# A fused adaLN, linear-attention and SwiGLU block: K-V state folded into the output projection, per-tile transposes, and the output projection spread over the first FFN chunk

## The chip, the cores and the metric

The kernel runs on one core of one Trainium2 chip. The metric is device time in microseconds (us). "Fast" runs are those within 1.5% of the fastest run of the same kernel; all times compared below are of fast runs.

The engines are TensorE (PE: matmuls; PEld: its weight loads, which overlap with matmuls, as 862.9 and 413.4 us of the two fit into a span of 915.7 in the kernel before), VectorE (DVE), ScalarE (ACT), GpSimd (POOL) and SyncE (SP, which issues most DMA here: 171 of the 235 issues of the kernel before). "Granted clock" (PEclk) is the share of full speed that the throttle gave TensorE. These kernels put matmul results into PSUM tiles, called banks here (a wide matmul's is 128x512 in f32); to evict one is to copy it out with another engine. A wide matmul is one with 512 columns.

## The reference

The input x is 2048 x 1024, and w_gate and w_up are 1024 x 3584. There are 32 heads of width 32. Everything is stored in bf16.

```python
mod = silu(c) @ w_mod                       # six rows of 1024: sa, ca, ga, sb, cb, gb
h = layernorm(x) * (1 + ca) + sa
q, k, v = split(h @ wqkv)
phi = lambda t: where(t > 0, t + 1, exp(t)) + 1e-6
kv  = einsum('bhsd,bhse->bhde', phi(k), v);  z = phi(k) summed over s
o   = (phi(q) @ kv) / (phi(q) . z + 1e-6)   # per head
x = x + ga * (o @ wo)
h = layernorm(x) * (1 + cb) + sb
x = x + gb * ((silu(h @ w_gate) * (h @ w_up)) @ w_down)
```

The order of the stages is forced. All of kv and z must be known before any output row. Each output row needs wo, then the second layer norm, then a transpose for the next matmul, and then the FFN.

## The kernel before

The 2048 rows are 16 tiles of 128, in 4 chunks of 512. In the first phase each chunk does a layer norm, K, V, Q and an update of kv. Then each tile does `nd` (numerator and denominator), a division, a transpose of o, the projection with wo, and the second layer norm. Tiles 4 to 15 are interleaved with gate and up of FFN chunk 0. The rest is an FFN stream.

```python
def emit_nd(st):                    # phi(q) @ [kv | z]: 8 matmuls, 132 columns
    ...
    nc.vector.reciprocal(out=rd[:], in_=rd[:])
    ...                             # o_sb = numerator * rd
def emit_tp(o_sb, st):              # 8 transposes of o, one eviction
    ...
def emit_wo(st, oT_t):
    ...                             # a_ps = oT_t @ wo (16 matmuls), x1 = x + a_ps, bn_stats
    nc.gpsimd.tensor_scalar(out=xn2[:], in0=x1_t[:], scalar1=rstd[:], scalar2=nmr[:], ...)
    xn2_lists.setdefault(sc, []).append(xn2)          # only collected here
    ...
    elif t == STC - 1:              # transposes when the chunk's four tiles are there
        transpose_chunk_to(h2T_c, xn2_lists[sc], cb1T, sbT, ...)

def p456_iter(i):                   # three tiles in flight
    o_tiles[i + 2] = emit_nd(i + 2)
    oT_tiles[i + 1] = emit_tp(o_tiles.pop(i + 1), i + 1)
    emit_wo(i, oT_tiles.pop(i))
...
interleave(ffn_gate_up_iter(0, gu_pool, psum_gu), list(range(STC, ST)))
```

## Time and profile before

| kernel before | us |
|---|---|
| median of 4 runs (beside the changed kernel) | 915.83 (914.19 to 917.9) |
| span of the profiled run | 915.7 |
| TensorE busy | 862.9 (94%) |
| VectorE / ScalarE / GpSimd busy | 303.3 / 212.2 / 58.1 |

TensorE bounds the kernel. Eight 128x512 matmuls take 1.73 us when they run unbroken (216 ns each), and from about 429 us on, the profile is an almost unbroken stream of them. A matmul's own record is longer (379 ns), so successive records overlap. For that reason a group's busy time can be read as a share, but the pace has to be read from the timeline.

The waits view of the kernel before, TensorE only, names the waiting instruction and its releaser, then us in total, times, and the longest.

```profile
PE mT_ps L175 <- DMA wme<-in_w_mod_dram: 18.4, 4, 10.0
PE acc L265 <- DVE pk_c L220: 6.8, 3, 3.3
PE y_ps L534 <- DMA wd_sb<-in_B_w_down_dram: 3.5, 3, 1.6
```

The start costs most: TensorE waits for w_mod, then for evictions of K. Two groups of the kernel before are work that the change removes. The columns are count, busy us, mean ns, and the idle time before them.

```profile
L363 PE MATMUL tp<-ident,o_sb 128*128 128x128 bf16 x128 | 11.3, 225 | 0.9 <-DVE o_sb L353 0.7
L340 PE MATMUL nd<-KVZ,pqT 128*128 128x132 bf16 x128 | 11.2, 226 | 1.3 <-DVE KVZ L312 1.2
```

### The profile page before, as it was taken

To read this page: it belongs to the slowest core of one execution; us is meant where nothing else is said; L and a number is where in the kernel's file an instruction comes from. 1 tells how busy PE (TensorE), PEld (TensorE's weight loads), DVE (VectorE), ACT (ScalarE), POOL (GpSimd) and SP (SyncE) were. 2 spreads that over 40 slices of the span, in tenths; PEclk is the share of its full clock that TensorE was granted. 3 is DMA by queue.
4 is the path that set the end of the run, shared out by engine and by line. 5 is a ranking of instruction groups with operands and counts; after the bars stand their busy time and mean duration, and the time that the engine had idled before them with its cause. 6 is when DMAs were issued, how large, how long until landed. Compare 5 with 4: busy or idle time off the path is not lost.

```text
span 915.7 us, 11358 instructions
## 1 busy us (share of the span) xinstructions
PE 862.9 (94%) x4672; PEld 413.4 (45%) x4760; DVE 303.3 (33%) x568; ACT 212.2 (23%) x362; POOL 58.1 (6%) x109
## 2 busy tenths in 40 slices
PE   1789999997999999998999999999999999999998
PEld 1335464444444544544444444444444444444443
DVE  4745255443665444441121222212212212122222
ACT  3526345342342422313011100111100111110000
POOL 2100000000422122120000000000000000000000
PEclk9999999998999999999999999999999999999999
DMA  9921060031215464459755542454531355511120
GB/s 330 393 104 47 4 227 1 1 92 35 104 66 158 122 184 142 123 151 352 227 153 158 149 127 70 143 158 142 155 110 61 101 157 152 143 48 64 69 69 24
DMA packets 153955, 117.13 MB, mean 128 GB/s; under 512 B 3888, under 2 KB 141104, under 8 KB 153904
## 3 DMA queue, kind: packets, MB, share of 16 engines
q1 hardware_dynamic: 144688, 91.24, 33.0%
q10 hardware_dynamic: 6912, 16.78, 5.8%
q0 software_dynamic: 2304, 8.39, 2.3%
q8 instruction: 37, 0.61, 0.3%
q14 instruction: 14, 0.11, 0.0%
HBM read 103.81 MB, written 12.58 MB: 127 GB/s over the span
## 4 chain that ended last, share of the span: by engine, by line
PE 68%; DMA 3%; DVE 2%; issue 1%; POOL 1%; ACT 1%; SPq 0%; POOLq 0%; DVEq 0%; ACTq 0%
PE y_ps L534 21%; PE u_ps L455 19%; PE g_ps L451 19%; PE a_ps L404 5%; DMA wd_sb<-in_B_w_down_dram 2%; PE tp L363 1%; ACT h2T_c L125 1%; PE nd L340 1%; DVE x_t L406 1%; DMA x_scratch<-x_t 1%; PE tp L121 1%; PE g_ps L398 0%; PE u_ps L226 0%; PE a_ps L398 0%; PE g_ps L226 0%
## 5 line engine op out<-in xcount | busy, mean ns | idle before, releaser
L455 PE MATMUL u_ps<-h2T_c,wu_blk 128*128 128x512 bf16 x877 | 212.1, 379 | 0.9
L451 PE MATMUL g_ps<-h2T_c,wg_blk 128*128 128x512 bf16 x880 | 212.2, 379 | 0.7
L534 PE MATMUL y_ps<-wd_sb,gu 128*128 128x512 bf16 x878 | 195.5, 381 | 4.4 <-DMA wd_sb<-in_B_w_down_dram 3.5
L464 DVE TENSOR_TENSOR gu<-u_ps,sg 128x512 bf16<-128x512 f32 x112 | 77.5, 692 | 296.0 <-PE u_ps L455 266.3
L458 ACT ACTIVATE sg<-g_ps 128x512 f32<-128x512 f32 x112 | 66.9, 598 | 428.8 <-PE g_ps L451 410.8
L534 PEld LDWEIGHTS <-gu 128*128 128x128 bf16 x896 | 88.0, 98 | 111.0 <-issue 6.5
L451 PEld LDWEIGHTS <-wg_blk 128*128 128x128 bf16 x896 | 87.4, 98 | 104.0 <-issue 0.2
L455 PEld LDWEIGHTS <-wu_blk 128*128 128x128 bf16 x896 | 87.3, 98 | 102.9
L265 PE MATMUL acc<-wkv_sb,hT_c 128*128 128x512 bf16 x373 | 88.0, 388 | 7.6 <-DVE pk_c L220 6.8
L537 DVE TENSOR_TENSOR yt<-y_ps,gb_bc 128x512 f32<-128x512 f32 x32 | 22.1, 692 | 155.2 <-PE y_ps L534 155.2
L265 PEld LDWEIGHTS <-hT_c 128*128 128x128 bf16 x384 | 37.5, 100 | 50.7 <-issue 9.9
L219 DVE TENSOR_SCALAR e<-e 128x512 f32<-128x512 f32 x56 | 23.6, 424 | 71.0 <-ACT e L218 71.0
L218 ACT ACTIVATE e<-acc 128x512 f32<-128x512 f32 x56 | 33.2, 603 | 54.4 <-PE acc L226 32.1
L404 PE MATMUL a_ps<-wo_sb,oT_t 128*128 128x512 bf16 x183 | 44.4, 379 | 1.3 <-DVE x_t L406 0.5
L226 PE MATMUL acc<-hT_c,wq_sb 128*128 128x512 bf16 x186 | 42.1, 379 | 0.3
L226 PEld LDWEIGHTS <-wq_sb 128*128 128x128 bf16 x256 | 24.4, 98 | 27.2 <-issue 0.5
L271 ACT CAST v_c<-acc 128x512 bf16<-128x512 f32 x32 | 18.7, 585 | 41.1 <-PE acc L265 39.3
L404 PEld LDWEIGHTS <-oT_t 128*128 128x128 bf16 x192 | 18.2, 97 | 22.2 <-issue 3.1
L265 PE MATMUL acc<-wkv_sb,hT_l 128*128 128x512 bf16 x124 | 28.0, 379 | 0.2
L102 DVE BATCH_NORM_STATS2 stats<-x_sb 128x6 f32<-128x512 bf16 x32 | 21.0, 670 | 9.2 <-DMA x_sb<-in_A_x_dram 9.2
L538 DVE TENSOR_TENSOR ob<-yt,x1r 128x512 bf16<-128x512 f32 x32 | 22.1, 692 | 1.1
L406 DVE TENSOR_TENSOR x_t<-a_ps,x_t 128x512 f32<-128x512 f32 x24 | 16.5, 687 | 17.7 <-PE a_ps L404 17.7
(216 smaller groups left out, 489.7 us busy)
## 6 DMA issues: line engine op xcount, KB each, us to landing
wg_blk<-in_B_w_gate_dram SPq DMA_DIRECT2D x56, 512.0 KB, 3.9
wu_blk<-in_B_w_up_dram SPq DMA_DIRECT2D x56, 512.0 KB, 5.0
wm_blk<-in_w_mod_dram SPq DMA_DIRECT2D x8, 1024.0 KB, 6.0
x_scratch<-x_t POOLq DMA_DIRECT2D x16, 512.0 KB, 3.9
x1r<-x_scratch ACTq DMA_DIRECT2D x16, 512.0 KB, 3.5
wd_sb<-in_B_w_down_dram SPq DMA_DIRECT2D x7, 1024.0 KB, 13.7
x_sb<-in_A_x_dram ACTq DMA_DIRECT2D x16, 256.0 KB, 6.2
wme<-in_w_mod_dram SPq DMA_DIRECT2D x4, 1024.0 KB, 12.4
```

The lines of the kernel that those rows point to most:

```text
L218: nc.scalar.activation(out=e[:], in_=acc, func=ACT.Exp)
L219: nc.vector.tensor_scalar(out=e[:], in0=e[:], scalar1=1.0, scalar2=PHI_EPS, op0=ALU.min, op1=ALU.add)
L226: nc.tensor.matmul(acc[:], lhsT=wq_sb[:, cc, qc * P:(qc + 1) * P], rhs=hT_[:, cc, :], start=(cc == 0), stop=(cc == DC - 1))
L265: nc.tensor.matmul(acc[:], lhsT=hT_c[:, cc, t * P:(t + 1) * P], rhs=wkv_sb[:, cc, n0:n0 + NB], start=(cc == 0), stop=(cc == DC - 1))
L404: nc.tensor.matmul(a_ps[:], lhsT=oT_t[:, cc, :], rhs=wo_sb[:, cc, nb * NB:(nb + 1) * NB], start=(cc == 0), stop=(cc == DC - 1))
L406: nc.vector.tensor_tensor(out=x1_t[:, nb * NB:(nb + 1) * NB], in0=a_ps[:], in1=x_t[:, nb * NB:(nb + 1) * NB], op=ALU.add)
L451: nc.tensor.matmul(g_ps[:, 0:width], lhsT=wg_blk[:, cc, fj * P:(fj + 1) * P], rhs=h2T_c[:, cc, cs], start=(cc == 0), stop=(cc == DC - 1))
L455: nc.tensor.matmul(u_ps[:, 0:width], lhsT=wu_blk[:, cc, fj * P:(fj + 1) * P], rhs=h2T_c[:, cc, cs], start=(cc == 0), stop=(cc == DC - 1))
L458: nc.scalar.activation(out=sg[:, 0:width], in_=g_ps[:, 0:width], func=ACT.Silu)
L464: nc.vector.tensor_tensor(out=gu[:, cs], in0=u_ps[:, 0:width], in1=sg[:, 0:width], op=ALU.mult)
L534: nc.tensor.matmul(y_ps[:], lhsT=guT[sc][f][:, t * P:(t + 1) * P], rhs=wd_sb[:, f, nb * NB:(nb + 1) * NB], start=(f == 0), stop=(f == FC - 1))
L537: nc.vector.tensor_tensor(out=yt[:], in0=y_ps[:], in1=gb_bc[:, nb * NB:(nb + 1) * NB], op=ALU.mult)
```

## The change

The aim is less TensorE work and an earlier start. It does the following:

- It folds the block-diagonal kv into wo once (16 matmuls, `wf`), so that `nd` and the 128 transposes of o disappear. phi(q) is divided by its denominator in place. The denominators of four head groups go into the four 32-column groups of one PSUM bank (`den`), and after a reciprocal, 8 selector matmuls (`bc`) spread them.
- It computes the late modulation rows as wide matmuls with 32 output columns, four column groups to a bank (`modr`).
- It loads x first, then w_mod and the K weights in pieces, and computes K of chunk 0 over six PSUM banks.
- It transposes each tile as soon as its rows are normalised (on VectorE), in both layer norms.
- It gives chunks 1 to 3 of the projection, with their denominators, to the first FFN chunk as side work.

```diff
-    def emit_nd(st): ...
-    def emit_tp(o_sb, st): ...
+    def den_norm(sc):
+        for k in range(2):
+            for g in range(4):
+                nc.tensor.matmul(den[32 * g:32 * g + 32, :], lhsT=Zden[:, 4 * k + g, :], rhs=pq[:, 4 * k + g, :], ...)
+        ...                                   # add eps, reciprocal 128x512, cast
+                nc.tensor.matmul(bc[:], lhsT=Esel[32 * g:32 * g + 32, k, :], rhs=rb[32 * g:32 * g + 32, :], ...)
+                nc.vector.tensor_tensor(out=pq[:, hg, :], in0=bc[:], in1=pq[:, hg, :], op=ALU.mult)
+    ...                                       # wf: wo <- KVT @ wo, 16 matmuls
+    def wo_tile(st):
+        ...                                   # a_ps = pq @ wo (16 matmuls), x1 = a_ps + x_t, bn_stats
+        normalise(xn[:], x1[:], mv[:, 0, 0:1], rstd[:, 0:1])
+        ...
+            pe_transpose_tile(h2Ts[sc], xn, t)        # in the same call
+        if t == STC - 1:
+            ...                               # scale and shift h2T
-        xn2_lists.setdefault(sc, []).append(xn2)
-        elif t == STC - 1:
-            transpose_chunk_to(h2T_c, xn2_lists[sc], cb1T, sbT, ...)
...
+    side = []                                 # wo_tile(4..15), den_norm(2), den_norm(3)
+    for fb in gate_up_blocks(0): ...          # one or two of them after each gate/up block
```

## The prediction

> **What bounds the kernel now.** TensorE: the page gives PE 862.9 of 915.7 us busy (94%), no other engine over 33%. The chain of waits shows eight 128x512 matmuls per 1.73 us (216 ns each); from about 428 to 911 us it is an unbroken stream of FFN matmuls, 2240 x 0.216 = 484 us. The change leaves that stream alone; gain or loss is before 428 us. There the windows show TensorE losing time in three places: 27.5 us idle in the first 60 us (waits view: 18.4 us for w_mod, 6.8 us for pk evictions; DMA full at 350-400 GB/s from 2 to 51 us; first K matmul at 26.4 us); some 10 us between 212 and 240 us, with granted clock 0.83; some 5 us at 430-437 us waiting for wd.
>
> **TensorE work, counted in the instruction order.**
> Removed: nd 128 (11.2 us busy), o transposes 128 (11.3), identity matmuls 8 (1.7), late matvecs 256 and their broadcasts (8.9): 33 us.
> Added (estimates at 216 ns per 512 columns): folded wo 16 (3.5 us), selector broadcasts 4+32 (7.8), KV transposes 8 (0.8), late mod rows 64 and denominators 32 with 32 output columns. If four column tiles run at once, [...] these 96 cost 24 x 0.216 = 5.2 us; if not, 20.7. No trace shows it yet; I expect overlap. Net about -15 us.
>
> **Start.** x comes first, then w_mod and K weights interleaved, 7 MB; pieces with 512 B runs go at about 285 GB/s (wg/wu: 155 GB/s at 0.55 DMA share), landing near 25 us. K of chunk 0 fills six banks as they land, done near 30 us. But chunk 1's normalisation stands ahead of phi on VectorE (about 7 us), and x loads, waiting for buffers, stand ahead of wv in the single SP queue; so K ends near 40 us and V starts near 41. At 69 us I expect about 190 wide matmuls done against 142 before: gain about 11 us.
>
> **Given back.** Before the first FFN: 16 folded-wo evictions on ScalarE (0.6 us each), the chain a_ps, add, BN_STATS, normalise, transpose (3.5-4.5 us) exposed on the last wo tile, then modulation; about 11 us idle, as before. In the first FFN each denominator chain has a 128x512 reciprocal (128x32 takes 351 ns; estimate 4 us), and eight products of 0.69 us pace the broadcasts: about 2 us idle for each of three chunks, plus 0.5-0.7 us at each of 12 transposes. wd should wait 0-2 us. These eat most of the removed work: the stage is about 3 us longer. Late mod: -4; kv evictions with four banks: -2; the rest: about -1.
>
> Sum: -11 +3 -4 -2 -1 = -15 us: **900 us**, range 887 to 914. Chances: faster by over 2% 0.40, within 2% 0.55, slower by over 2% 0.05.
>
> **What would show it.** Right: wide matmuls at 216 ns, the stream after the first down projection as long as before; at least 10 us less idle in the first 60; late-mod and denominator matmuls nearer 54 than 216 ns apart; small waits on pq products and xn transposes; VectorE up by about 50 us to 350.
> Wrong: column tiles at 216 ns (+10 to 15 us); V waiting beyond 45 us for wv; the first FFN over 8 us longer, waiting on VectorE; gate/up waiting for weights because x1r and output DMAs share their queue.
>
> **What would make it wrong.** Another DMA rate at the start, VectorE saturating in the first FFN, or a clock drop after idles (0.83, 0.74 seen before).

The sum: -11 + 3 - 4 - 2 - 1 = -15 us, from 915.7 to about 900. The 5.2 us for 96 overlapping matmuls, in the count of TensorE work, was the expectation; no trace showed it then.

## More of the kernel before

A tile's normalised rows are put on a list, and the transposes of all four tiles of a chunk are emitted only after the projection of the fourth. (What ran stands in places in another order than the source emits it: transposes of `xn_2429` ran at 239.59 us, before the chunk's last projection matmuls at 248.44. So the order is read from the timelines.)

Now the end of one chunk's projection in the timeline of the kernel before. The columns are start, length, engine, line, operation, tiles and count, and in brackets the idle time just before.

```profile
304.58 1.89 PE L404 MATMUL a_ps<-wo_sb,oT_t 128*128 128x512 bf16 x7
306.30 1.24 PE L451 MATMUL g_ps<-h2T_c,wg_blk 128*128 128x512 bf16 x5
307.38 1.89 PE L455 MATMUL u_ps<-h2T_c,wu_blk 128*128 128x512 bf16 x8
309.11 1.03 PE L451 MATMUL g_ps<-h2T_c,wg_blk 128*128 128x512 bf16 x4
310.86 0.28 PE L121 MATMUL tp<-ident,xn_3223 128*128 128x128 bf16 x2 [0.73 <-POOL xn_3223 L421]
```

Between the last projection matmul of the chunk (`a_ps`) and the first transpose of its fourth tile (`xn_3223`) stand 17 gate and up matmuls. They cover most of the normalisation, and TensorE waits 0.73 us.

The windows view of the kernel before, from the last update of kv (215.6 us) to the first matmul of the down projection (429.03), gives busy us and instructions of each engine, then the granted clock. I call this stretch the middle.

```profile
215.60:429.03 213.43, 203.23 (x1170) 101.56 (x1192) 101.83 (x194) 69.36 (x141) 46.88 (x82) 0.98 0.45 140
```

TensorE is busy for 203.23 of 213.43 us: 10.2 us idle.

## The result, and the profile after

The changed kernel took 927.03 us (median of 4 runs, 924.51 to 929.28) against 915.83 for the kernel before. The ratio is 1.012, 95% interval 1.009 to 1.0151: the same at 2%, but slower and not faster, and outside the predicted range. A ratio here is the mean time of one kernel's fast runs over that of the other's of the same rounds, so it is not quite the ratio of the medians. The experiments' ratios are all to the kernel before, which took 916.4 to 917.5 us, so kernels are best compared by ratio. The profiled run of the changed kernel is the slowest of its four: 929.28 us at a mean granted clock of 0.982, where the fastest took 924.51 us at 0.989.

TensorE is 94% busy again (867.4 of 927.6 us). So that share tells nothing of where the time went. The spans of the profiles, cut at two events, do tell it. The first cut of this table is the start of the last kv matmul; the windows views begin at its end, 0.2 us later.

| us | to the last update of kv | from there to the first down matmul (middle) | from there to the end | span |
|---|---|---|---|---|
| before | 215.4 | 213.6 | 486.7 | 915.7 |
| after | 194.3 | 242.7 | 490.6 | 927.6 |

Two pieces of work lie on different sides of the cuts. The changed kernel leaves 96 matmuls of Q for the middle, the kernel before 64. The kernel before had 32 gate/up matmuls of chunk 1 behind it at its first down matmul: its weight loads after that cut are 656 + 656, where three chunks need 1,344. Each difference is 32 x 0.216 = 6.9 us. With both corrected, the first part is 14.2 us shorter, the middle 29.1 us longer (the two corrections cancel there), and the last part 3.0 us shorter: 11.9 us longer in all. So the start went nearly as hoped, and everything was lost in the middle.

The windows view of the changed kernel for its middle:

```profile
194.50:436.98 242.48, 211.48 (x998) 91.57 (x1016) 146.94 (x259) 45.34 (x78) 18.21 (x32) 0.93 0.44 134
```

TensorE is idle for 31.0 us instead of 10.2, and the granted clock is 0.93 instead of 0.98. Busy time also rose by 8.2 us, although matmuls were removed.

The waits view of the changed kernel, TensorE only:

```profile
PE tp L181 <- DVE xn L172: 35.6, 16, 10.1
PE mod_ps L212 <- DMA wme<-in_w_mod_dram: 3.8, 3, 2.2
PE bc L377 <- DVE pq L380: 2.5, 7, 0.8
PE acc L444 <- DMA wgu<-in_B_w_gate_dram: 1.8, 3, 0.7
...
PE acc L239 <- DVE pk L225: 1.4, 2, 1.1
PE bc L377 <- ACT rb L373: 1.3, 1, 1.3
```

The start improved as intended (w_mod 18.4 to 3.8, K evictions 6.8 to 1.4). But transposes now wait 35.6 us for normalised rows. Of these, 12.8 us lie at the very start, before any rows are there, and 22.8 us in the middle.

The groups of the changed kernel:

```profile
L410 PE MATMUL a_ps<-wo,pq 128*128 128x512 bf16 x249 | 68.1, 430 | 1.0 <-DVE pq L380 0.5 <-issue 0.2
L300 PE MATMUL modr<-wml,sc_122 128*32 128x512 bf16 x64 | 4.6, 381 | 0.0
L367 PE MATMUL den<-pq,Zden 128*32 128x512 bf16 x32 | 2.7, 413 | 0.0
L371 DVE RECIPROCAL e<-e 128x512 f32<-128x512 f32 x4 | 13.4, 3349 | 0.0
```

A wide matmul of the output projection has a mean of 430 ns, where the other large wide groups have 379 to 389: some ran at a lower clock (16 from 235.17 us on took 5.30 us, at a granted clock of 0.50 up to 238.6). The column-tiled matmuls are short (64 in 4.6 us; 29 of them in a row from 77.24 to 79.07 us, 63 ns apart), as predicted.

The timeline of the changed kernel around tiles 1, 2 and 3:

```profile
234.71 0.65 PE L181 MATMUL tp<-ident,xn 128*128 128x128 bf16 x8 [2.75 <-DVE xn L172]
235.17 5.30 PE L410 MATMUL a_ps<-wo,pq 128*128 128x512 bf16 x16
243.91 0.62 PE L181 MATMUL tp<-ident,xn 128*128 128x128 bf16 x8 [3.44 <-DVE xn L172]
244.37 3.62 PE L410 MATMUL a_ps<-wo,pq 128*128 128x512 bf16 x15
251.43 0.62 PE L181 MATMUL tp<-ident,xn 128*128 128x128 bf16 x8 [3.45 <-DVE xn L172]
```

The 16 projection matmuls of tiles 2 and 3 are followed directly by that tile's own transposes, with nothing between; tile 1 has 4 Q matmuls there. At 235.17, after a wait of 2.75 us, a block of 16 takes 5.30 us; at 244.37, after one of 3.44 us, it takes 3.62. What TensorE waits for is a chain on VectorE, here of the tile projected at 235.17, in the changed kernel's VectorE timeline:

```profile
240.51 0.69 DVE L412 TENSOR_TENSOR x_2316<-a_ps,x_sb 128x512 f32<-128x512 f32 x1 [0.31 <-PE a_ps L410]
241.23 0.69 DVE L413 BATCH_NORM_STATS2 stats<-x_2316 128x6 f32<-128x512 f32 x1
241.96 0.21 DVE L416 BATCH_NORM_AGGREGATE mv<-stats 128x2 f32<-128x12 f32 x1
242.20 0.15 DVE L160 TENSOR_SCALAR veps<-mv 128x1 f32<-128x1 f32 x1
243.04 0.81 DVE L172 TENSOR_SCALAR xn<-x_2316,mv,rstd 128x1024 bf16<-128x1024 f32 x1 [0.69 <-POOL rstd L162]
```

From the last projection matmul to the normalised rows it is 3.4 us, for a tile that needs 3.45 us of matmuls. Six tiles have this: 1, 2 and 3, and the first tile of each later chunk (4, 8, 12), with 2.75, 3.44, 3.45, 3.53, 3.51 and 3.51 us. The other tiles of the later chunks have some 15 or more gate and up matmuls between and wait at most 0.28 us, but for tile 11 with 0.74. Tile 0 has Q matmuls.

The page of the changed kernel has TensorE busy and its clock in 40 slices of 23 us, in tenths:

```profile
PE   3799999999589989799999999999999999999998
PEclk9999999999879989799999999999999999999999
```

The dents in both rows are in the middle, and a lower clock is beside lower busy time. Cut finer, the windows view shows a granted clock of 0.50 in the slow stretches, from 235.2 to 238.6 us and from 254.35 to 258.5.

### The profile page after: what moved, and what is told of

Its sections match the earlier page's. It is cut to its first block, busy times and chain, and to the rows that moved or that the text cites. A ratio compares the mean times of both kernels' runs of the same rounds, so it can differ in the third digit from the quotient of the medians.

```text
span 927.6 us, 10537 instructions
## 1 busy us (share of the span) xinstructions
PE 867.4 (94%) x4312; PEld 398.4 (43%) x4396; DVE 362.0 (39%) x669; ACT 158.8 (17%) x271; POOL 34.4 (4%) x86
## 4 chain that ended last, share of the span: by engine, by line
PE 80%; DVE 10%; DMA 3%; SPq 2%; ACT 1%; issue 1%; POOL 1%; POOLq 0%; ACTq 0%; DVEq 0%
PE acc L464 21%; PE acc L448 18%; PE acc L444 18%; PE a_ps L410 6%; PE acc L253 6%; PE acc L264 4%; PE acc L239 4%; DVE xn L172 1%; PE tp L181 1%; DVE stats L413 1%; SPq L115 1%; DMA wgu<-in_B_w_gate_dram 1%; DVE e L371 1%; DVE pq L380 1%; POOL rstd L162 1%
## 5 line engine op out<-in xcount | busy, mean ns | idle before, releaser
L444 PE MATMUL acc<-h2T,wgu 128*128 128x512 bf16 x876 | 212.3, 381 | 4.2 <-DMA wgu<-in_B_w_gate_dram 1.8
L448 PE MATMUL acc<-h2T,wgu 128*128 128x512 bf16 x879 | 213.6, 380 | 1.2 <-issue 0.2
L464 PE MATMUL acc<-wd,gu 128*128 128x512 bf16 x878 | 193.1, 379 | 0.9
L452 DVE TENSOR_TENSOR gu<-acc,e 128x512 bf16<-128x512 f32 x112 | 77.3, 690 | 268.4 <-PE acc L448 256.5
L451 ACT ACTIVATE e<-acc 128x512 f32<-128x512 f32 x112 | 66.9, 597 | 488.8 <-PE acc L444 473.5
L444 PEld LDWEIGHTS <-wgu 128*128 128x128 bf16 x896 | 87.5, 98 | 111.5 <-issue 5.9
L448 PEld LDWEIGHTS <-wgu 128*128 128x128 bf16 x896 | 87.2, 98 | 106.4 <-issue 3.0
L410 PE MATMUL a_ps<-wo,pq 128*128 128x512 bf16 x249 | 68.1, 430 | 1.0 <-DVE pq L380 0.5
L239 PE MATMUL acc<-wk,hT 128*128 128x512 bf16 x246 | 58.9, 389 | 2.3 <-DVE pk L225 1.4
L264 PE MATMUL acc<-hT,wq 128*128 128x512 bf16 x248 | 58.1, 379 | 0.4
L253 PE MATMUL acc<-wv,hT 128*128 128x512 bf16 x252 | 55.9, 379 | 0.4 <-DMA wv<-in_A_wqkv_dram 0.2
L181 PE MATMUL tp<-ident,xn 128*128 128x128 bf16 x256 | 21.6, 240 | 35.8 <-DVE xn L172 35.6
L223 ACT ACTIVATE e<-acc 128x512 f32<-128x512 f32 x64 | 38.0, 601 | 96.1 <-PE acc L239 51.2
L410 PEld LDWEIGHTS <-pq 128*128 128x128 bf16 x256 | 27.5, 109 | 38.0 <-issue 15.8
L239 PEld LDWEIGHTS <-hT 128*128 128x128 bf16 x256 | 24.8, 99 | 32.6 <-issue 5.4
L253 PEld LDWEIGHTS <-hT 128*128 128x128 bf16 x256 | 25.0, 98 | 30.0 <-issue 0.3
```

The lines of the kernel that those rows point to most:

```text
L181: nc.tensor.transpose(tp[:, cc, :], xn[:, cc * P:(cc + 1) * P], ident[:])
L223: nc.scalar.activation(out=e[:], in_=acc, func=ACT.Exp)
L239: nc.tensor.matmul(acc[:], lhsT=hTs[sc][:, cc, t * P:(t + 1) * P], rhs=wk[cc // 4][:, cc % 4, nb * NB:(nb + 1) * NB], start=(cc == 0), sto ...
L253: nc.tensor.matmul(acc[:], lhsT=hTs[sc][:, cc, t * P:(t + 1) * P], rhs=wv[cc // 4][:, cc % 4, nb * NB:(nb + 1) * NB], start=(cc == 0), sto ...
L264: nc.tensor.matmul(acc[:], lhsT=wq[cc // 4][:, cc % 4, qc * P:(qc + 1) * P], rhs=hTs[sc][:, cc, :], start=(cc == 0), stop=(cc == DC - 1))
L410: nc.tensor.matmul(a_ps[:], lhsT=pq[:, hg, t * P:(t + 1) * P], rhs=wo[hg // 4][:, hg % 4, ns], start=(hg == 0), stop=(hg == HG - 1))
```

## The experiments

Theory A: the transposes directly behind their own matmuls expose the VectorE chain six times, and the gaps make the throttle lower the clock of what follows. Theory B: the middle waits for data, as x loads that wait for a buffer hold the one SyncE queue for tens of us (four of them for 39.23 us from 231.85 on), with gate and up weights behind them. Theory C: VectorE (362.0 us busy, up from 303.3) is overloaded by the denominators, and the chain is long only for that.

### e1: the x loads of the projection on another queue

```diff
-        nc.sync.dma_start(out=x_t[:], in_=x2[st * P:(st + 1) * P, :])
+        nc.scalar.dma_start(out=x_t[:], in_=x2[st * P:(st + 1) * P, :])
```

> The x tiles of the output projection are loaded through ScalarE's queue, so that the gate/up weights no longer stand behind them; TensorE's instruction order stays as it was. Theory A (the layernorm chain of a tile is exposed because its transposes stand right behind its own matmuls, and the idle then halves the clock): the order is unchanged, so the six waits of 2.7 to 3.5 us stay, 925 to 928 us. Theory B (the waits come from gate/up weights arriving late in the single queue): the three waits in the first FFN go with their slow matmuls, about 908 to 912 us.

Measured: 928.92 us (927.32 to 930.21), ratio 1.0119 (1.0091 to 1.0146), just as the changed kernel. The transposes wait 34.9 us as before. Theory B falls as the main cause.

### e2: each tile's transposes one tile later

```diff
-        if t == 0: h2Ts[sc] = ... ; pe_transpose_tile(...) ; modulate   # at the end of wo_tile
+        return sc, t, xn
+    def wo_back(sc, t, xn): ...                                         # those lines, as a call of their own
+    pend = []
+    def wo_step(st):
+        pend.append(wo_tile(st))
+        if len(pend) > 1:
+            wo_back(*pend.pop(0))
...                                       # wo_step called in place of wo_tile; what is left in pend is flushed after Q and at the end
```

> The transposes of a tile are emitted one tile later, nothing else. Theory A: the six waits on xn of 2.7 to 3.5 us (20 us) and the slow matmuls after them (about 10 us) go, 895 to 900 us, VectorE as busy as before. Theory C (VectorE is the limit of the first FFN, through reciprocals, products and normalisation): the waits move to other places, 920 us or more.

Measured: 890.99 us (890.72 to 894.42), ratio 0.9715 (0.9686 to 0.9743), correct. The same instructions in another order are 36 us faster than the changed kernel (medians), and 2.85% faster than the kernel before. The timeline of e2 around the same tiles, and its windows view for the middle:

```profile
230.09 0.62 PE L181 MATMUL tp<-ident,xn 128*128 128x128 bf16 x8
230.55 3.62 PE L410 MATMUL a_ps<-wo,pq 128*128 128x512 bf16 x16
234.01 0.61 PE L181 MATMUL tp<-ident,xn 128*128 128x128 bf16 x8
234.45 3.62 PE L410 MATMUL a_ps<-wo,pq 128*128 128x512 bf16 x16
```

```profile
197.30:401.70 204.40, 198.31 (x1017) 88.53 (x1015) 140.77 (x251) 44.61 (x77) 18.41 (x32) 0.99 0.54 167
```

A transpose finds its rows ready, because another tile's 16 matmuls ran meanwhile. (For tile 3 it was 18 of the last Q matmuls; in the changed kernel 17 of these ran behind tile 0.) The middle is 38.1 us shorter than in the changed kernel: 24.9 us less idle (31.0 to 6.1) and 13.2 us less busy time (211.48 to 198.31) for the same work. Theory A holds for the waits, and about a third of the loss was matmuls that took longer, at a lower clock (0.93 in the changed kernel's middle, 0.99 here). Whether the gaps are what lowers the clock is for e8. One slow stretch is left in e2: the 32 projection matmuls after the broadcasts of chunk 1 take 8.75 us. e12 ran the same kernel again:

> e2 once more, unchanged, on the same chip as e9, e10 and e11, to compare a few microseconds without the difference between chips: ratio to the kernel before 0.969 to 0.974, near 891 us.

Measured: 891.79 us (890.54 to 892.94), ratio 0.972 (0.9701 to 0.9739). It repeats.

### e3: a shorter chain (wrong result)

```diff
-        normalise(xn[:], x1[:], mv[:, 0, 0:1], rstd[:, 0:1])
+        nc.vector.tensor_scalar(out=xn[:], in0=x1[:], scalar1=neg_half[:], scalar2=neg_half[:], op0=ALU.subtract, op1=ALU.mult)
```

> Wrong result on purpose: the second normalisation uses constants in place of mean and rstd, so the transposes wait for a shorter chain (no aggregate, no rstd); order of TensorE nearly as it was. Theory A: each of the six waits falls from 3.5 to about 1.5 us and the clock no longer halves after them: 12 us + 10 us less, about 905 us. Theory D (the clock falls for another reason than these idles): only 12 us less, about 915, with slow matmuls still there.

Measured: 911.62 us (909.27 to 913.45), ratio 0.9922 (0.9891 to 0.9953). The second layer norm uses constants, so its statistics leave the chain. The six waits shrank together to 11.5 us (2.23 to 2.25 us each, except the first with 0.29). The gain of about 15 us (17 against e1) goes in A's direction but is smaller than A expected, because the clock still fell (0.90 from 212 to 262 us, 0.96 from there to 300). The timeline of e3:

```profile
239.20 0.62 PE L181 MATMUL tp<-ident,xn 128*128 128x128 bf16 x8 [2.23 <-DVE xn L419]
239.66 5.30 PE L410 MATMUL a_ps<-wo,pq 128*128 128x512 bf16 x16
```

A block of 16 projection matmuls takes 5.30 us right after a wait of only 2.23 us. So a slow block did not need a gap of 3.4 us here. Slow matmuls still there are also what theory D foretold (the clock falls for another reason than these gaps). e3 alone does not decide between A and D; e8 does for the blocks behind the gaps.

### e4: without the denominators of chunks 1 to 3 (wrong result)

```diff
-    den_norm(1)
...
-        if sc + 1 < NSC:
-            side.append(lambda s=sc + 1: den_norm(s))
```

> Wrong result on purpose: the denominators of chunks 1 to 3 (sums, reciprocals, broadcasts, products) are left out. Theory A: only their own cost goes, 3 x (0.6 + 1.7 us of TensorE and 1 to 1.5 us of waits), about 915 to 918 us, and the long waits behind tiles 4, 8 and 12 stay. Theory C (VectorE congestion by the denominators makes those waits): these three waits go too, about 900 us.

Measured: 908.12 us (905.52 to 909.45), ratio 0.9889 (0.986 to 0.9919). The timeline of e4 at tiles 4 and 8:

```profile
270.14 0.62 PE L181 MATMUL tp<-ident,xn 128*128 128x128 bf16 x8 [3.55 <-DVE xn L172]
270.60 3.62 PE L410 MATMUL a_ps<-wo,pq 128*128 128x512 bf16 x16
...
317.95 0.62 PE L181 MATMUL tp<-ident,xn 128*128 128x128 bf16 x8 [3.51 <-DVE xn L172]
318.40 3.62 PE L410 MATMUL a_ps<-wo,pq 128*128 128x512 bf16 x16
```

The waits are as long as ever without the denominators' VectorE work, so theory C falls. It gained more than was expected, and the clock accounts for it: after these waits it did not fall (3.62 us for the next 16, at tile 12 too), and the granted clock from 262 to 430 us stayed at 1.00. The four slow blocks that the changed kernel has in its later chunks cost it 9.1 us. A single gap of 3.5 us between dense stretches was not enough here. In the changed kernel the same gaps come only 16 matmuls after the eight `bc` matmuls of the chunk, which e4 does not have; that this makes the difference is not shown. Tiles 1 to 3 are as in the changed kernel, with a block of 5.30 us behind tile 1's wait.

### e5: K of chunk 0 not over six banks

```diff
-    k_phase(0, True)
+    k_phase(0, False)
```

on e2.

> The deferred-transpose version (e2) with the K matmuls of chunk 0 over one bank at a time, as in the later chunks, instead of over six banks. The prediction counted the six banks into an 11 us gain at the start. Theory 'the six banks buy the early start': without them the first K matmuls stall on each next piece of the K weights and the start gets 4 to 8 us longer, 895 to 899 us. Theory 'the gain at the start comes from loading x first and the K weights in pieces, and the transposed rows': K matmuls begin only when the last w_mod piece has landed anyway, so few matmuls run ahead, and the time stays within 3 us of e2, 888 to 894.

Measured: 889.98 us (887.74 to 891.16), ratio 0.9701 (0.9674 to 0.9728), against 0.9715 for e2. The six banks buy nothing that can be measured here (the intervals overlap). In e2 only 5 of the 64 K matmuls of chunk 0 ran before the last matmuls on w_mod, at 27.11 us. The earlier start comes from the rest of the rewrite of the start; which piece of that gives how much was not taken apart further.

### e6: column groups one after the other

```diff
-        for j in range(DC):
-            for g in range(4):
+        for g in range(4):
+            for j in range(DC):
```

on e2, and likewise for the denominators.

> The deferred-transpose version (e2) with the late modulation rows (64 matmuls) and the denominators (32) issued column group by column group, so that consecutive matmuls hit the same 32 columns. If the four column groups run side by side in the changed kernel (the late modulation took 4.6 us busy for 64), this ordering takes it away: 64 at about 216 ns are 13.8 us, 9 us more, and the denominators 2 to 4 us more, so 900 to 904 us. If the short time per matmul has another cause (32 output columns alone), nothing changes: 889 to 893.

Measured: 897.47 us (896.64 to 898.44), ratio 0.9787 (0.9757 to 0.9816): slower than e2, but by less than expected. The group of e6:

```profile
L300 PE MATMUL modr<-wml,sc 128*32 128x512 bf16 x64 | 11.1, 380 | 0.3
```

The 64 modulation matmuls take 11.1 us instead of 5.0 in e2. The 32 of the denominators stay at 2.5 us, as in e2. So the column groups do overlap here, and how much depends on the order of issue: 5.0 us with the group changing each time, 11.1 with eight in a row to one group. With only two in a row (the denominators) no loss showed.

### e7: all x, x1 and out transfers on the ScalarE queue

```diff
-        load_x(st, nc.sync)                                   # and in wo_tile, down
+        load_x(st, nc.scalar)
```

on e2.

> The deferred-transpose version (e2) with the loads of x and x1 and the stores of out on the ScalarE queue instead of the SyncE queue, which keeps the weights alone. If gate and up starts wait for their weights because an x, x1 or out transfer stands ahead of them in the one queue, the waits for wgu (about 3 us in e2) and for wv (1.6 us) go and the time falls by 2 to 5 us, 886 to 889. If they wait for buffers of the weight pool instead, nothing falls, 889 to 893; if transfers that wait for VectorE now block ScalarE's own work, it is slower.

Measured: 895.15 us (894.41 to 897.06), ratio 0.9764 (0.9738 to 0.979): slower than e2. The waits for gate and up weights did go, but a new wait came at the start. A line of the waits view of e7, and two from its VectorE timeline:

```profile
PE mod_ps L212 <- DVE hT L184: 7.1, 1, 7.1
```

```profile
17.31 0.64 DVE L168 BATCH_NORM_STATS2 stats<-x_sb 128x6 f32<-128x512 bf16 x1
...
25.00 1.41 DVE L184 COPY hT<-tp 128x512 bf16<-128x512 bf16 x4
```

With a queue of their own, x rows of the next chunk land early: VectorE has its first statistics of them at 14.52 us, where in e2 it still waits for them until 29.08. In e7 it does that chunk's statistics (14.5 to 25 us) before it evicts the transposes that TensorE needs. In e2 the x loads stand behind weights in the one queue, and those evictions begin at 15.14 us. The one queue had been setting the right order.

### e8: useless matmuls in the six gaps of the changed kernel

```diff
+        if st in (1, 2, 3, 4, 8, 12):
+            dm = acc_b("dummy")
+            for i in range(14):
+                nc.tensor.matmul(dm[:], lhsT=ident[:], rhs=wo[0][:, 0, 0:NB], start=(i == 0), stop=(i == 13))
```

before the transposes in `wo_tile`, on the changed kernel and not on e2.

> The changed kernel itself (not e2) with 14 useless 128x512 matmuls (3.0 us) put into the six places where the transposes of an output-projection tile stand directly behind its own matmuls. It does no less work and the chain on VectorE is as long; only the idle of TensorE is filled. Theory 'the idle gaps also lower the granted clock afterwards': the six waits shrink below 1 us, the clock from 212 to 438 us stays near 1.00 and the time falls by about 10 to 16 us, 911 to 917, although 84 matmuls were added. Theory 'the clock falls for another reason (load of VectorE or DMA)': the waits are merely replaced by work and the time stays at 924 to 930.

Measured: 922.08 us (921.18 to 922.68), ratio 1.0053 (1.0029 to 1.0078), against 1.012 for the changed kernel. With 84 matmuls of useless work (84 x 0.216 = 18.1 us) it is some 5 us faster. The six waits are now 0.2 to 0.5 us, and no projection block behind one of them is slow any more: each takes 3.62 us or less, where in the changed kernel those behind tiles 1, 4, 8 and 12 take 5.30, 6.20, 6.16 and 5.91. So the gaps did lower the clock of what followed them. The gain missed the expected 10 to 16 us because the clock still fell twice (blocks of 5.30 us at 262.32 and of 5.76 at 371.26), not after a long gap but after the denominators' broadcasts. The timeline of e8:

```profile
260.53 0.37 PE L377 MATMUL bc<-rb,Esel 32*128 32x512 bf16 x1 [0.23 <-DVE pq L380]
261.13 0.37 PE L377 MATMUL bc<-rb,Esel 32*128 32x512 bf16 x1 [0.23 <-DVE pq L380]
261.73 0.37 PE L377 MATMUL bc<-rb,Esel 32*128 32x512 bf16 x1 [0.23 <-DVE pq L380]
262.32 5.30 PE L410 MATMUL a_ps<-wo,pq 128*128 128x512 bf16 x16 [0.23 <-DVE pq L380]
```

Eight `bc` matmuls with short waits before and between them, paced by VectorE (2.4 us idle of the last 4.3), were enough to make the next 16 take 5.30 us. In the changed kernel too, one of the slow blocks (at 377.92) stands right behind such broadcasts and not behind a transpose.

### e9: only the late transfers on the ScalarE queue

As e7, but with the x loads of the first phase left on SyncE.

```diff
-        nc.sync.dma_start(out=x_t[:], in_=x2[st * P:(st + 1) * P, :])      # likewise x1r and out in down
+        nc.scalar.dma_start(out=x_t[:], in_=x2[st * P:(st + 1) * P, :])
```

> The deferred-transpose version with only the late transfers moved to the ScalarE queue: x for the output projection, x1 for the second FFN half, the stores of out. The x loads of the first phase stay where they were, since in e7 their early landing let VectorE take chunk 1's statistics first, which delayed the first evictions by 7 us. If gate and up starts had waited for transfers standing ahead of their weights, the waits for wgu (2 to 3 us in e2) go and the time is 2 to 3 us under the repeated e2 (e12). If not, the two are equal within 1 us.

Measured: 888.63 us (888.13 to 889.8), ratio 0.9688 (0.9669 to 0.9706), 3.2 us under e12. No wait for gate or up weights is left among TensorE's. The 8.75 us for the 32 matmuls behind the broadcasts of chunk 1 are still there. So theory B was right about a cost of about 3 us, after the main cause was gone, though not about the main cause.

### e10: the first denominators behind a gate/up block

```diff
-    den_norm(1)
     gen = gate_up_blocks(0)
-    side = []
+    side = [lambda: den_norm(1)]
...
-        want = min(nside, -(-nside * (fb + 1) // (NFB - 2)))
+        want = min(nside, nside * (fb + 1) // (NFB - 2))
```

on e9.

> e9 with the denominators of chunk 1 moved behind the first gate/up block and the output-projection tiles spread a little further, so that the eight broadcasts have gate/up matmuls between them. In e2 they had small waits (1.4 us together) and the 32 matmuls after them took 8.75 us instead of 6.9. If sparse work on TensorE is what lowers the granted clock, both go: 2 to 4 us under e9, 884 to 887 us. If the slow stretch has nothing to do with the broadcasts, it shows up elsewhere and the gain is under 1.5 us.

Measured: 886.13 us (885.85 to 886.76), ratio 0.9658 (0.964 to 0.9676), correct. It is 2.5 us under e9 and the best version: 3.4% faster than the kernel before. The clock row of e10's page, its windows view for the middle, and its projection matmuls:

```profile
PEclk9999999999999999999999999999999999999999
```

```profile
196.00:397.00 201.00, 196.63 (x1018) 87.88 (x1016) 141.17 (x251) 44.38 (x77) 18.42 (x32) 1.00 0.50 157
```

```profile
L410 PE MATMUL a_ps<-wo,pq x256: 378/379/379, 221.1 to 382.0; 128*128 128x512 bf16 x128
```

Every projection matmul is at 378 or 379 ns (minimum, median, maximum), and the clock over the middle is 1.00. With the broadcasts between dense matmuls, the slow stretch is gone. Against e9's profile the middle has 1.7 us less busy time (198.32 there) and 1.6 us less idle. The edit also spreads the projection tiles, which was not tested apart. And one of e9's four runs had a mean clock of 1.00 as well and took 888.13 us, so the clock need not be the larger part of the 2.5 us.

### e11: transposes deferred for the first four tiles only

```diff
-            side.append(lambda st=sc * STC + t: wo_step(st))
+            side.append(lambda st=sc * STC + t: wo_back(*wo_tile(st)))
```

on e2.

> The changed kernel with the transposes deferred only for the first four output-projection tiles; tiles 4, 8 and 12 keep their transposes directly behind their own matmuls. If each of the six waits costs its length plus the slow stretch after it, this removes 9.6 us of waits and one slow stretch of 1.7 us, and keeps 10.6 us of waits and 8.6 us of slow stretches: 914 to 917 us. If the first four alone put the later stage into its bad rhythm, it comes near e2 (891 to 896); if they did not matter, it stays at 925 to 929.

Measured: 913.87 us (911.01 to 919.32), ratio 0.9968 (0.9941 to 0.9994), about 13 us under the changed kernel and 22 above e12. The gaps add up: taking away those of tiles 1 to 3 gives over a third of e2's gain, those of tiles 4, 8 and 12 with their slow stretches the rest.

## Why the prediction was wrong

The prediction was 900 us; the result was 927.

- **What bounds the kernel** (TensorE; all gain or loss before the FFN stream): right. The last part changed by 3.0 us only, at equal work, about the 3.5 us that the kernel before waits there for the weights of the down projection.
- **The start** (gain of 11 by 69 us, then late modulation 4, kv evictions 2 and the rest 1: 18 in all): right in kind, too large. Measured: 14.2 us at equal work. At 69 us the changed kernel had issued 176 weight loads of K, V and Q against 146, which is 6.5 us at 0.216, where 190 against 142 were foretold; TensorE's idle time in the first 60 us fell by 8.3 us (27.5 to 19.2), not by at least 10. The later terms gave the other 7.7 us, and 7 were foretold. That the six banks were part of the reason is not supported by e5.
- **Column tiles overlap**: right. The trace shows 64 matmuls of 512 columns in 4.6 us and 29 of them 63 ns apart (foretold: nearer 54 than 216), and e6 takes it away by order alone (11.1 us).
- **The denominators** (a reciprocal of 4 us by estimate, and about 2 us idle for each of three chunks): the reciprocal took 3.35 us, and TensorE was idle before the broadcasts for 2.5 us on pq products and 1.3 us on the cast after the reciprocal, 3.8 where 6 were foretold. Right in mechanism, too large by a third.
- **VectorE up by about 50 us to 350**: 362.0. Right, and e4 shows that this load was not the trouble.
- **"Given back"**: this is the step that failed. It took the chain of add, statistics, normalise and transpose (put at 3.5 to 4.5 us, which was right: for the tile shown, 3.4 us to the normalised rows and 4.1 to the end of the transposes) as exposed only on the last projection tile before the FFN, with 0.5 to 0.7 us at each of the 12 later transposes, and "the stage is about 3 us longer". The middle is 29.1 us longer. The chain was exposed on six tiles, not one, for 20.2 us of waits. The order of instructions, from which the prediction took its counts, holds this: 16 projection matmuls, 8 transposes of the same tile, 16 projection matmuls. The prediction does not ask what stands between a producer and its consumer. e2, which emits the transposes one tile later and changes nothing else, makes the middle 9.0 us shorter than in the kernel before (204.6 against 213.6) where the changed kernel has it 29.1 longer.
- **The clock**: the prediction named "a clock drop after idles" as something that would make it wrong, but gave it no size. In the middle the changed kernel's busy time is 13.2 us above e2's for the same work, and five blocks of projection matmuls took 1.7 to 2.6 us too long each. The traces show what such stretches look like: the granted clock is 0.50 in the changed kernel's, from 235.2 to 238.6 us and from 254.35 to 258.5; e8 and e9 have a slow stretch right behind broadcasts with waits of 0.23 us between them (5.30 us for 16, 8.75 for 32); e10, where other matmuls stand between the broadcasts, has none. The same loss recurs: the changed kernel, e3, e4 and e8 each have a block of 16 that took 5.30 instead of 3.62 us, 1.68 more. What sets this length is not shown.
- **Weights behind other transfers in one queue**, also named as a risk: real and small, about 3 us (e9).

Where the expected gain went is therefore settled: the rest of the rewrite gains more than the 15 us foretold (e2 is 26 us under the kernel before by its ratio), and the position of the transposes, with the clock that followed, took back all of it and more. What stays open is the exact condition under which the throttle lowers the clock. A gap of 3.51 us was followed by a slow block in the changed kernel (tile 8, 6.16 us for 16) and not in e4 (3.62); within the changed kernel one of 2.75 us was (5.30) and one of 3.44 us was not (3.62); one of 2.23 us was in e3 (5.30); in e8 and e9 gaps of 0.23 to 0.75 us between the broadcasts were (5.30 for 16, 8.75 for 32).

## What to carry to other kernels

When a change replaces a batched step by a per-tile one, look in the order of instructions of the bounding engine at how much independent work stands between a tile's last matmul and the first instruction that needs its result through another engine; a chain of 3.5 us needs some 16 wide matmuls there (16 x 0.216 = 3.5). Emitting the consumer one tile later costs no work (and here no further buffer), and it was worth 36 us. Count a gap on TensorE at more than its length, as matmuls after a gap or a sparse stretch can also be slower (here 5.30 to 6.20 us for 16 in place of 3.62), and do not trust the busy share: 94% stood beside both 916 and 927 us. The share of the weight loads does not rank these kernels either: 45% before (span 915.7 us), 43% after (927.6), 44% in e2 (892.7), 45% in e10 (885.1).
